# Attention and dense layers with urgent chains, and reciprocals spread to features by DMA

## The chip, the cores and the metric

The kernel runs on one core of one Trainium2 chip. The metric is the device time of one execution in microseconds (us). The kernel before takes 293.84 us, the median of three runs (293.66 to 294.12). TensorE multiplies matrices, VectorE (DVE) and ScalarE (ACT) work on elements, GpSimd (POOL) does small jobs, and SyncE (SP) issues DMAs. Each engine runs its instructions in order and waits on semaphores for the others. Matmuls write to PSUM, which has 8 banks of 128 x 512 f32.

## The reference

x is 2048 tokens by 512 features, bf16. Two blocks alternate, A, B, A, B, with the same weights both times:

```python
x = x + _A_ref(_layernorm(x), wqkv, wo)   # linear attention, 32 heads of 16
x = x + _B_ref(_layernorm(x), w1, w2)     # relu(x @ w1) @ w2, hidden 1376

# _A_ref:
phi = lambda t: jnp.where(t > 0, t + 1, jnp.exp(t)) + 1e-6
pq, pk = phi(q), phi(k)
kv = einsum("bhsd,bhse->bhde", pk, v);  z = einsum("bhsd->bhd", pk)
num = einsum("bhqd,bhde->bhqe", pq, kv)
den = einsum("bhqd,bhd->bhq", pq, z)[..., None] + 1e-6
return (num / den) @ wo
```

The layer norm has no weights and an epsilon of 1e-5.

## The kernel before, in words

Tokens are 16 tiles of 128, in four chunks of four tiles. Everything stays in SBUF: the f32 residual `xres`, the normalized `xn`, its transpose `Tb`, and `big`, which holds phi(k), phi(q) and later the hidden layer.

An attention layer has these parts. `a_k` multiplies `Tb` by wk for a tile and `phi_evac` (L502) evicts it: ScalarE writes x + 1 (L506) and exp (L508), VectorE takes the minimum with 1 (L510) and the maximum of both (L516). `a_q` does the same for q, but transposed: features in partitions, 512 tokens of a chunk in columns. `a_z` sums phi(k) by matmuls with a column of ones. `a_g` accumulates xn^T phi(k) in four banks (`g`), evicted as `GT`; `a_kv` turns this into k^T v with the weights wv, so v itself is never computed. `a_m` masks it to the heads' blocks (`KVT`, L582) and multiplies by wo, which gives the 512 x 512 matrix `Mf`, evicted in four parts (L589). `a_fin` then makes an output tile with four matmuls, phi(q) by `Mf`, and `resid` (L534) adds it to the residual and sums it; L540 on ScalarE sums its squares.

The division is done on phi(q), before `a_fin`. `a_den` (L602) multiplies by `Zc`, so that the denominators of 32 heads lie in 32 rows for each j (of four groups of 128 features), and ScalarE forms the reciprocal as exp(-ln), `rdc` (L608, L610). Only 8 of the 32 rows of a group are heads of it. `a_pqs` (L613) spreads a reciprocal to its head's 16 features with a matmul by a 0/1 matrix, `Esel`, four matmuls of 32 rows for a chunk into four banks, and VectorE multiplies phi(q) by that bank (L619). `Esel` itself is made once at the start by `head_rows` (L427).

A dense layer has `b_h` (10 slices of 128 hidden features for a chunk, relu at L641), `b_hl` for the last 96 features, and `b_group`, in which a group of four tiles begins with matmuls of 32 rows (`w2l`) and goes on with ten for each tile (`w2`).

The norm between layers is `ln_chunk` (L442): four small VectorE operations, a power on GpSimd (L459), one more on VectorE (L461), and `ln_norm` (L464) on ScalarE, VectorE or GpSimd. The transposes of a chunk are one DMA transpose issued by SP (L480), which waits for the four tiles' norms and, the first time, for all loads. Chunk 0 of the dense layers, and chunks 0 and 1 of the first, are transposed on TensorE instead (L485), so that the next layer can begin earlier.

The order is not written out by hand. `layer_steps` lists the steps of each layer and interleaves the end of one layer with the start of the next; every operation goes into a graph with its reads, writes and an assumed duration, and `_list_schedule` (L117) simulates the engines and picks for each, within a window of its next operations, the one that can start first (ties by program order). It also hands out the eight PSUM banks. Operations that may run on several engines (`add_flex`) go where they would end first. The result is a fixed list of instructions for each engine. The assumed durations (L16 to L38) therefore change the order, though not the work.

Of the kernel before, what the change touches and what calls it, by code (L numbers as in the profile page):

```python
# [16 lines left out]
C_MM128 = 58.0  # L17
# [14 lines left out]
C_POOL_POW = 1000.0  # L32
C_POOL_NORM = 900.0
C_SP_ISSUE = 60.0
TAIL = {PE: 70.0, ACT: 230.0, DVE: 80.0, POOL: 300.0, SP: 0.0}
SYNC_LAT = 40.0
LN_EXP_SET = 6
WINDOW = {PE: 64, ACT: 80, DVE: 80, POOL: 12, SP: 6}  # L38


class _Op:
    __slots__ = ("eng", "emit", "reads", "writes", "dur", "lat", "sdeps", "odeps", "idx",
                 "seq", "dma", "name", "t_start", "t_done", "issued", "pos", "nsucc", "alts")
# [19 lines left out]
class _Graph:  # L63

    def __init__(self):
        self.ops = []
        self.last_w = {}
        self.readers = {}
        self.tile_ops = {}
        self.ntiles = 0  # L70

# [5 lines left out]
    def add(self, eng, emit, reads=(), writes=(), dur=100.0, lat=0.0, dma=False, name=""):  # L77
        op = _Op(eng, emit, tuple(reads), tuple(writes), dur, lat, dma, name)
        op.idx = len(self.ops)
        deps = {}  # L80
# [36 lines left out]
def _list_schedule(ops, tile_ops, vbank, nbanks=8):  # L117
# [15 lines left out]
    pend = {e: [o for o in ops if e in engs_of(o)] for e in ENGINES}  # L133
# [4 lines left out]
    remaining = len(ops)  # L138

    def ready_time(o):  # L140
        t = 0.0
        for d in o.sdeps:
            if d.t_done is None:
                return None
            if d.t_done + SYNC_LAT > t:
                t = d.t_done + SYNC_LAT
        for d in o.odeps:
            if not d.issued:
                return None
        need = alloc_of.get(o.idx)  # L150
        if need:
            fr = sorted(x for x in bank_free if x is not None)
            if len(fr) < len(need):
                return None
            tb = fr[len(need) - 1] + SYNC_LAT
            if tb > t:
                t = tb
        return t

    while remaining:  # L160
        best = None
        for e in ENGINES:
# [33 lines left out]
            if cand is not None and (best is None or cand[0] < best[0] - 1e-9  # L196
                                     or (abs(cand[0] - best[0]) <= 1e-9 and cand[1].idx < best[1].idx)):
                best = cand
# [45 lines left out]
def build_kernel(nc, A_x, A_wqkv, A_wo, B_w1, B_w2, out, n_layers_pairs=2, K_STT=0, Q_STT=0, A_PE_CHUNKS=1, windows=None,  # L244
                 WARM=16, SPLIT0=True, TAIL_SPLIT=True, LAST_HALVES=True, FIRST_PE_CHUNKS=2,
# [22 lines left out]
    with es:  # L268
# [15 lines left out]
        NL = 2  # L284
        lnd = sb("lnd", [128, NL, 512], F32)
# [3 lines left out]
        Esel = sb("Esel", [128, 128], BF16)  # L289
# [11 lines left out]
        nm2 = sb("nm2", [128, NT], F32)  # L301
        var = sb("var", [128, NT], F32)
# [6 lines left out]
        veps0 = sb("veps0", [128, 1], F32)  # L309
        rstd0 = sb("rstd0", [128, 1], F32)  # L310
        nbias0 = sb("nbias0", [128, 1], F32)
# [28 lines left out]
        def dma(emit, reads, writes, xfer_ns, name):  # L340
# [5 lines left out]
            op = g.add(SP, _emit, reads, writes, dur=C_SP_ISSUE, lat=xfer_ns, dma=True, name=name)  # L346
# [23 lines left out]
        def h_keys(c):  # L370
            return [("big", il * RU + c) for il in range(4)]
# [3 lines left out]
        def ld_x(t, lo=0):  # L375
            dma(lambda e, t=t: e.dma_start(xin[:, 4 * t + lo:4 * t + 4, :], x_v[:, 4 * t + lo:4 * t + 4, :]),
                [], [("xin", i) for i in range(4 * t + lo, 4 * t + 4)], 1500.0 * (4 - lo) / 4.0, "ld_x%d" % t)
        dma(lambda e: e.dma_start(xin[:, 0, :], x_v[:, 0, :]), [], [("xin", 0)], 450.0, "ld_x0a")
        wq_v = A_wqkv.rearrange("(c p) n -> p c n", p=128)
        ld_x(0, 1)  # L380
        dma(lambda e: e.dma_start(wqkv[:, :, D:2 * D], wq_v[:, :, D:2 * D]), [], [("wk",)], 1500.0, "ld_wk")  # L381
        dma(lambda e: e.dma_start(wqkv[:, :, 0:D], wq_v[:, :, 0:D]), [], [("wq",)], 1500.0, "ld_wq")  # L382
        for t in range(1, NCH):
            ld_x(t)
# [36 lines left out]
        ones_v = onesf[:, :].rearrange("p (j r) -> p j r", r=32)  # L421
        g.add(POOL, lambda e: e.affine_select(hm1[:], ones_v, [[0, 4], [-16, 32]], ALU.is_ge, 0.0, base=0, channel_multiplier=1),
              [("onesf",)], [("hm1",)], 350, name="as_h1")
        g.add(POOL, lambda e: e.affine_select(hm128[:], hm1[:], [[0, 4], [16, 32]], ALU.is_ge, 0.0, base=15, channel_multiplier=-1),
              [("hm1",)], [("hm128",)], 350, name="as_h2")

        def head_rows():  # L427
            b = alloc_bank()
            g.add(PE, lambda e: e.transpose(psv[:, b, 0:64].bitcast(BF16), hm128[:].rearrange("p j r -> p (j r)"), ident[:]),
                  [("hm128",), ("ident",)], [("ps", b)], C_MM128, name="trh")  # L430
            g.add(DVE, lambda e: e.tensor_copy(Esel[:], psv[:, b, 0:64].bitcast(BF16)), [("ps", b)], [("Esel",)], 200.0, name="esel")
# [6 lines left out]
        def ln_stats_first(i):  # L438
            g.add(DVE, lambda e: e.bn_stats(bst[:, i, :], xin[:, i, :]), [("xin", i)], [("bst", i)], C_DVE_BNST, name="bnst%d" % i)  # L439
            g.add(DVE, lambda e: e.bn_aggr(mv[:, i, :], bst[:, i, :]), [("bst", i)], [("mean", i), ("var", i)], C_DVE_SMALL, name="bnag%d" % i)  # L440

        def ln_chunk(t, first):  # L442
            sl = slice(4 * t, 4 * t + 4)
            tl = range(4 * t, 4 * t + 4)
            if first:
                mean_ap = mv[:, sl, 0]
                g.add(DVE, lambda e: e.tensor_scalar(veps[:, sl], mv[:, sl, 1], 0.0, EPS, ALU.max, ALU.add),
                      [("var", i) for i in tl], [("veps", t)], C_DVE_SMALL, name="veps%d" % t)
            else:
                mean_ap = mean[:, sl]  # L450
                g.add(DVE, lambda e: e.tensor_scalar(mean[:, sl], s1[:, sl], INV_D, None, ALU.mult),
                      [("s1", i) for i in tl], [("mean", i) for i in tl], C_DVE_SMALL, name="mean%d" % t)
                g.add(DVE, lambda e: e.scalar_tensor_tensor(nm2[:, sl], mean[:, sl], -1.0, mean[:, sl], ALU.mult, ALU.mult),
                      [("mean", i) for i in tl], [("nm2", t)], C_DVE_SMALL, name="nm2_%d" % t)
                g.add(DVE, lambda e: e.scalar_tensor_tensor(var[:, sl], s2[:, sl], INV_D, nm2[:, sl], ALU.mult, ALU.add),
                      [("s2", i) for i in tl] + [("nm2", t)], [("var", i) for i in tl], C_DVE_SMALL, name="var%d" % t)
                g.add(DVE, lambda e: e.tensor_scalar(veps[:, sl], var[:, sl], 0.0, EPS, ALU.max, ALU.add),  # L457
                      [("var", i) for i in tl], [("veps", t)], C_DVE_SMALL, name="veps%d" % t)
            g.add(POOL, lambda e: e.tensor_tensor(rstd[:, sl], veps[:, sl], nhalf[:, 0:4], ALU.pow),  # L459
                  [("veps", t), ("nhalf",)], [("rstd", t)], C_POOL_POW, name="rstd%d" % t)  # L460
            g.add(DVE, lambda e: e.scalar_tensor_tensor(nbias[:, sl], mean_ap, -1.0, rstd[:, sl], ALU.mult, ALU.mult),  # L461
                  [("mean", i) for i in tl] + [("rstd", t)], [("nbias", t)], C_DVE_SMALL, name="nbias%d" % t)

        def ln_norm(i, first):  # L464
            t = i // 4
            k = tile_of(i)
            src = xin[:, k, :] if first else xres[:, k, :]
            skey = ("xin", k) if first else ("xres", k)
            rd = [skey, ("rstd", t), ("nbias", t)]
            alts = [(ACT, lambda e: e.activation(xn[:, i, :], src, ACTF.Identity, scale=rstd[:, i:i + 1], bias=nbias[:, i:i + 1]),  # L470
                     C_ACT_SB_AP),
                    (DVE, lambda e: e.tensor_scalar(xn[:, i, :], src, rstd[:, i:i + 1], nbias[:, i:i + 1], ALU.mult, ALU.add),  # L472
                     C_DVE_NORM_BF if first else 460.0)]
            if not first:
                alts.append((POOL, lambda e: e.tensor_scalar(xn[:, i, :], src, rstd[:, i:i + 1], nbias[:, i:i + 1], ALU.mult, ALU.add),
                             C_POOL_NORM))
            g.add_flex(alts, rd, [("xn", i)], name="norm%d" % i)

# [23 lines left out]
        def phi_evac(b, dst_ap, dst_key, name, stt):  # L502
            s = scr_state["e"]
            scr_state["e"] = (s + 1) % NSCR
            if not stt:
                g.add(ACT, lambda e: e.activation(dst_ap, psv[:, b, :], ACTF.Identity, bias=1.0 + 1e-6, scale=1.0),  # L506
                      [("ps", b)], [dst_key], C_ACT_PSUM, name=name + "_lin")
# [4 lines left out]
            if stt:  # L512
                g.add(DVE, lambda e: e.scalar_tensor_tensor(dst_ap, psv[:, b, :], 1.0 + 1e-6, emscr[:, s, :], ALU.add, ALU.max),
                      [("ps", b), ("emscr", s)], [dst_key], C_DVE_PSUM, name=name + "_phi")
            else:
                g.add(DVE, lambda e: e.tensor_tensor(dst_ap, dst_ap, emscr[:, s, :], ALU.max),  # L516
                      [dst_key, ("emscr", s)], [dst_key], 340.0, name=name + "_phi")
# [25 lines left out]
        def a_k(i):  # L543
# [3 lines left out]
            phi_evac(b, pk_tile(i), ("big", pk_unit(i)), "k%d" % i, stt=(i % 4) < K_STT)  # L547

        def a_z(i, ZB):
# [4 lines left out]
            mm_group(mk, [("big", pk_unit(i)), ("ones1",)], [("ps", ZB)], 4 * C_MMTINY, "z%d" % i)  # L554
# [5 lines left out]
        def a_g(m, i0, GB):  # L560
# [7 lines left out]
            mm_group(mk, [("xn", i) for i in range(i0, i0 + 4)] + [("big", pk_unit(i)) for i in range(i0, i0 + 4)],  # L568
                     [("ps", GB)], 4 * C_MM512, "g%d_%d" % (m, i0 // 4))

        def a_g_evac(m, GB):
            g.add_flex([(ACT, lambda e: e.activation(GT[:, m, :], psv[:, GB, :], ACTF.Identity), C_ACT_PSUM),
                        (DVE, lambda e: e.tensor_copy(GT[:, m, :], psv[:, GB, :]), C_DVE_FLEX)],
                       [("ps", GB)], [("GT", m)], name="gev%d" % m)

# [5 lines left out]
        def a_m(KB):  # L581
# [393 lines left out]
```

## Time and profile before

| | |
|---|---|
| Median of the runs | 293.84 us (293.66 to 294.12) |
| Profiled execution | 294.0 us, of which the span, from first to last instruction, is 292.3 us |
| Granted TensorE clock | 0.999 |
| TensorE busy | 283.3 us, 97% |
| VectorE, ScalarE, GpSimd busy | 153.4, 172.5, 31.8 us |
| Idle time in front of matmuls, by what ended it | VectorE's memset of the warm-up 1.2, ScalarE's Tb 1.1, Mf 0.8, VectorE's big 0.4, its xn 0.3 us; 1.3 us in eight short pieces with no wait shown |
| DMA | 15.97 MB; all loads have landed by 24.87 us |

The profile is of one execution. Busy times are of instructions, so an engine that waits inside a long one looks busy, and TensorE's matmuls overlap: the mean of one is 379 ns, while the next starts 216 ns after it. The starts in the timeline are therefore a better measure than the sums. "Idle before" is what the engine waited for in front of a group; idle time of an engine that does not set the end costs nothing.

### The profile page before, as it was taken

The numbers are of one execution on the slowest core, as the hardware profiler recorded it, in microseconds if no ns is written. First come the engines' busy times: TensorE is split into PE (matmuls) and PEld (weight loads), VectorE is DVE, ScalarE is ACT, GpSimd is POOL, SyncE is SP. The second block draws the span as 40 slices with busy tenths as digits, with TensorE's granted clock in tenths as the row PEclk, the third lists the DMA queues.
The fourth block names the chain that finished last, engine by engine and source line by source line (L and its number), as shares of the span: only waits on it lengthen the run. The fifth ranks groups of instructions, "written<-read, shape, count | busy, mean of one in ns | idle before, by whom it ended". The sixth has DMA issues, their size and how long they took to land.

```text
span 292.3 us, 4292 instructions
## 1 busy us (share of the span) xinstructions
PE 283.3 (97%) x1649; PEld 128.7 (44%) x1670; DVE 153.4 (52%) x438; ACT 172.5 (59%) x354; POOL 31.8 (11%) x42
## 2 busy tenths in 40 slices
PE   7899999999999999999999999999999999999996
PEld 3354444334444444444444443444444444444443
DVE  5899774999940000347464758928994000022223
ACT  2998596687866664335644899258786766300000
POOL 3102100002430000022020300000243000000000
PEclk9999999999999999999999999999999999999999
DMA  7995320000370000030303400000038000001222
GB/s 222 357 374 107 63 27 0 2 0 0 72 147 0 0 2 0 3 72 11 61 2 72 72 3 0 2 0 0 3 64 152 1 2 0 2 9 63 72 74 72
DMA packets 33780, 15.97 MB, mean 55 GB/s; under 512 B 25312, under 2 KB 33248, under 8 KB 33760
## 3 DMA queue, kind: packets, MB, share of 16 engines
q1 hardware_dynamic: 33760, 15.70, 21.8%
q8 instruction: 13, 0.21, 0.3%
q14 instruction: 7, 0.06, 0.1%
HBM read 7.31 MB, written 2.10 MB: 32 GB/s over the span
## 4 chain that ended last, share of the span: by engine, by line
PE 88%; DVE 6%; DMA 2%; ACT 2%; issue 1%; SPq 1%
PE ps L523 87%; DMA xin<-in_A_x_dram 2%; DVE big L619 2%; DVE xn L472 1%; DVE xres L534 1%; ACT Mf L589 1%; ACT big L506 1%; PE ps L494 0%; DVE bst L439 0%; DVE big L516 0%; DVE emscr L510 0%; ACT sqscr L540 0%; SPq L382 0%; ACT escr L508 0%; SPq L381 0%
## 5 line engine op out<-in xcount | busy, mean ns | idle before, releaser
L523 PE MATMUL ps<-Tb,w 128*128 128x512 bf16 (+1 forms) x416 | 75.0, 379 | 0.0
L523 PE MATMUL ps<-w,big 128*128 128x512 bf16 (+1 forms) x321 | 69.2, 372 | 1.3 <-issue 1.3
L641 ACT ACTIVATE big<-ps 128x512 bf16<-128x512 f32 x78 | 46.5, 596 | 19.6 <-PE ps L523 19.6
L523 PEld LDWEIGHTS ps<-Tb,w 128*128 128x128 bf16 (+1 forms) x416 | 33.5, 97 | 41.2 <-ACT big L641 1.7
L523 PEld LDWEIGHTS ps<-w,big 128*128 128x128 bf16 x330 | 31.4, 98 | 37.6 <-issue 2.3
L534 DVE SCALAR_TENSOR_TENSOR xres<-ps,xres 128x512 f32<-128x512 f32 x32 | 21.8, 687 | 47.2 <-PE ps L523 46.9
L540 ACT ACTIVATE sqscr<-xres 128x512 bf16<-128x512 f32 x48 | 29.9, 629 | 27.5 <-DVE xres L534 27.3
L506 ACT ACTIVATE big<-ps 128x512 bf16<-128x512 f32 x64 | 40.9, 643 | 7.6 <-PE ps L523 7.3
L508 ACT ACTIVATE escr<-ps 128x512 bf16<-128x512 f32 x64 | 41.3, 661 | 0.4 <-DVE emscr L510 0.4
L531 DVE TENSOR_TENSOR xin<-ps,xres 128x512 bf16<-128x512 f32 x15 | 10.4, 692 | 54.5 <-PE ps L523 54.5
L459 POOL TENSOR_TENSOR rstd<-veps,nhalf 128x4 f32<-128x4 f32 x15 | 16.1, 1072 | 175.9 <-DVE veps L457 155.8
L523 PE MATMUL ps<-Tb,wqkv 128*128 128x512 bf16 x128 | 30.6, 379 | 0.0
L523 PE MATMUL ps<-wqkv,Tb 128*128 128x512 bf16 x124 | 28.8, 379 | 1.5 <-ACT Tb L498 1.1
L523 PE MATMUL ps<-Mf,big 128*128 128x512 bf16 x126 | 28.9, 380 | 1.1 <-ACT Mf L589 0.8
L523 PE MATMUL ps<-big,xn 128*128 128x512 bf16 x124 | 29.7, 379 | 0.3
L516 DVE TENSOR_TENSOR big<-big,emscr 128x512 bf16<-128x512 bf16 x64 | 26.5, 422 | 1.2
L510 DVE TENSOR_SCALAR emscr<-escr 128x512 bf16<-128x512 bf16 x64 | 18.5, 296 | 12.3 <-ACT escr L508 12.1
L619 DVE TENSOR_TENSOR big<-big,ps 128x512 bf16<-128x512 bf16 x32 | 19.9, 680 | 1.3 <-PE ps L523 1.3
L523 PEld LDWEIGHTS ps<-wqkv,Tb 128*128 128x128 bf16 x128 | 12.1, 98 | 16.0 <-ACT Tb L498 1.5
L523 PEld LDWEIGHTS ps<-Mf,big 128*128 128x128 bf16 x128 | 11.9, 98 | 16.2 <-ACT Mf L589 1.3
L523 PEld LDWEIGHTS ps<-big,xn 128*128 128x128 bf16 x128 | 11.5, 97 | 13.1 <-issue 1.5
L523 PEld LDWEIGHTS ps<-Tb,wqkv 128*128 128x128 bf16 x128 | 11.5, 97 | 12.3 <-DVE big L619 0.4
(71 smaller groups left out, 184.6 us busy)
## 6 DMA issues: line engine op xcount, KB each, us to landing
wqkv<-in_A_wqkv_dram SPq DMA_DIRECT2D x3, 512.0 KB, 6.1
xin<-in_A_x_dram SPq DMA_DIRECT2D x3, 512.0 KB, 8.0
out_dram<-xin SPq DMA_DIRECT2D x3, 512.0 KB, 2.9
w<-in_B_w_dram SPq DMA_DIRECT2D x1, 1376.0 KB, 11.0
w<-in_B_w_dram SPq DMA_DIRECT2D x1, 1280.0 KB, 13.7
wo<-in_A_wo_dram SPq DMA_DIRECT2D x1, 512.0 KB, 8.8
xin<-in_A_x_dram SPq DMA_DIRECT2D x1, 384.0 KB, 3.3
w2l<-in_B_w_dram SPq DMA_DIRECT2D x4, 96.0 KB, 7.6
```

The source lines that it names most:

```text
L459: g.add(POOL, lambda e: e.tensor_tensor(rstd[:, sl], veps[:, sl], nhalf[:, 0:4], ALU.pow), [("veps", t), ("nhalf",)], [("rstd", t)], C_POO ...
L472: (DVE, lambda e: e.tensor_scalar(xn[:, i, :], src, rstd[:, i:i + 1], nbias[:, i:i + 1], ALU.mult, ALU.add), C_DVE_NORM_BF if first else 4 ...
L506: g.add(ACT, lambda e: e.activation(dst_ap, psv[:, b, :], ACTF.Identity, bias=1.0 + 1e-6, scale=1.0), [("ps", b)], [dst_key], C_ACT_PSUM, ...
L508: g.add(ACT, lambda e: e.activation(escr[:, s, :], psv[:, b, :], ACTF.Exp), [("ps", b)], [("escr", s)], C_ACT_EXP, name=name + "_exp")
L510: g.add(DVE, lambda e: e.tensor_scalar(emscr[:, s, :], escr[:, s, :], 1.0, 1e-6, ALU.min, ALU.add), [("escr", s)], [("emscr", s)], C_DVE_B ...
L516: g.add(DVE, lambda e: e.tensor_tensor(dst_ap, dst_ap, emscr[:, s, :], ALU.max), [dst_key, ("emscr", s)], [dst_key], 340.0, name=name + "_ ...
L523: last = e.matmul(o, l, r, start=st, stop=sp, skip_group_check=skip)
L531: g.add(DVE, lambda e: e.tensor_tensor(xin[:, i, :], psv[:, b, :], src, ALU.add), [("ps", b), skey], [("xin", i)], C_DVE_PSUM, name="resid ...
L534: g.add(DVE, lambda e: e.scalar_tensor_tensor(xres[:, i, :], psv[:, b, :], 0.0, src, ALU.add, ALU.add, accum_out=s1[:, si:si + 1]), [("ps" ...
L540: g.add(ACT, lambda e: e.activation(sqscr[:, q, :], xres[:, i, :], ACTF.Square, accum_out=s2[:, si:si + 1]), [("xres", i)], [("sqscr", q), ...
L619: g.add(DVE, lambda e, j=j, u=u: e.tensor_tensor(unit_ap(u), unit_ap(u), psv[:, bs[j], :], ALU.mult), [("ps", bs[j]), ("big", u)], [("big" ...
L641: g.add_flex([(ACT, lambda e: e.activation(h_evac_ap(c, t), pin(), ACTF.Relu), C_ACT_PSUM), (DVE, lambda e: e.tensor_scalar(h_evac_ap(c, t ...
```

## The change

Seven things change together.

- The reciprocals are spread by DMA. The rows that `a_den` makes now hold each of a group's 8 heads four times (`hm128` repeats a head in 4 columns), so 32 rows hold 8 heads. `a_spread` copies each row to four partitions, four DMAs for a chunk into `rdx`, which has room for two chunks. `a_pqs` multiplies SBUF by SBUF. `head_rows`, `Esel` and the spreading matmuls go.
- The steps around the attention's middle (`bar`) are written in another order, with `a_den`, `a_spread` and `a_pqs` apart from each other and the q chunks between them.
- The output tiles of chunk 0 are made together by `a_fin4`, j outermost.
- Operations can be urgent: `g.urg` moves an operation ahead in the ranking of its engine (not on TensorE). The evictions of `GT`, the mask and `Mf`, the chain of chunk 0's norm and the last chunk's chain have it. One PSUM bank is held in reserve for the next operation in program order that needs one.
- `b_group` is split, and the `w2l` matmuls of the next group are put ahead of the last tile of the one before. Keys of `big` are now for quarters of a unit, so an output tile waits only for its own chunk's relu.
- The small operations of `ln_chunk` are all on GpSimd; the norms are on VectorE, with ScalarE as the alternative for the last two of a chunk. In the first chunk each tile has its own deviation, from Ln and Exp on ScalarE; in the others of the first layer the fourth norm is on ScalarE.
- The loads: x in pieces of 1, 1, 2 and 4 tiles, then wq, with wk issued by ScalarE; 12 warm-up matmuls instead of 16.

```diff
-C_POOL_POW = 1000.0
-C_POOL_NORM = 900.0
+C_POOL_POW0 = 420.0
+C_POOL_POW1 = 145.0
+C_POOL_SMALL = 150.0
...
+        op.urg = self.urg if eng != PE else 0
...
+    def rank(o):
+        return o.idx - o.urg
+    ranked = sorted(ops, key=rank)
...
+            if o is not hd and len(fr) < len(need) + min(RESERVE, len(alloc_of[hd.idx])):
                 return None
...
+        ld_x(0, 1)
+        ld_qk(D, "wk", ACT)
+        ld_x(1, 2)
+        ld_x(2, 4)
+        ld_x(4, 8)
+        ld_qk(0, "wq")
...
+        def ln_rstd_act(i):
+            g.add(ACT, lambda e: e.activation(veps[:, i:i + 1], mv[:, i, 1:2], ACTF.Ln, bias=EPS, scale=1.0),
...
+            g.add(ACT, lambda e: e.activation(rstd[:, i:i + 1], veps[:, i:i + 1], ACTF.Exp, scale=-0.5),
...
+        def ln_chunk(t):
...
+            g.add(POOL, lambda e: e.tensor_scalar(mean[:, sl], s1[:, sl], -INV_D, None, ALU.mult),
+            g.add(POOL, lambda e: e.tensor_tensor(nm2[:, sl], mean[:, sl], mean[:, sl], ALU.mult),
+            g.add(POOL, lambda e: e.tensor_scalar(ex2[:, sl], s2[:, sl], INV_D, None, ALU.mult),
+            g.add(POOL, lambda e: e.tensor_tensor(var[:, sl], ex2[:, sl], nm2[:, sl], ALU.subtract),
+            g.add(POOL, lambda e: e.tensor_scalar(veps[:, sl], var[:, sl], 0.0, EPS, ALU.max, ALU.add),
+            g.add(POOL, lambda e: e.tensor_tensor(rstd[:, sl], veps[:, sl], nhalf[:, 0:4], ALU.pow),
+            g.add(POOL, lambda e: e.tensor_tensor(nbias[:, sl], mean[:, sl], rstd[:, sl], ALU.mult),
...
+        def a_spread(t):
+            for j in range(4):
+                dma(lambda e, j=j: e.dma_start(rdx[:, t % NRD, j, :], rdc[32 * j:32 * j + 32, t, :].unsqueeze(1).broadcast_to([32, 4, 512])),
+                    [("rdc", t)], [("rdx", t % NRD, j)], 500.0, "rdx%d_%d" % (t, j), issue=600.0)
...
-            bs = [alloc_bank() for _ in range(4)]
-            mm_group(lambda: [(psv[:, bs[j], :], Esel[32 * j:32 * j + 32, :], rdc[32 * j:32 * j + 32, t, :], True, True, False) for j in range(4)],
...
-                g.add(DVE, lambda e, j=j, u=u: e.tensor_tensor(unit_ap(u), unit_ap(u), psv[:, bs[j], :], ALU.mult),
+                g.add(DVE, lambda e, j=j, u=u: e.tensor_tensor(unit_ap(u), unit_ap(u), rdx[:, t % NRD, j, :], ALU.mult),
...
+        def a_fin4(t, first_layer):
+            bs = [alloc_bank() for _ in range(4)]
+            for j in range(4):
+                u = pq_unit(j, t)
+                for il in range(4):
...
                 def o_step(il):
-                    b_group(il, last_layer)
+                    b_main(il, last_layer, 0, 3)
+                    if il < 3:
+                        b_small(il + 1, last_layer)
+                    b_main(il, last_layer, 3, 4)
```

## Prediction

> **What bounds the kernel now.** I read the page's busy shares first, then the chain that ended last, then TensorE's groups by shape, then the timeline around each stretch in which the chain leaves TensorE.
>
> ```profile
> PE 283.3 (97%) x1649; PEld 128.7 (44%) x1670; DVE 153.4 (52%) x438; ACT 172.5 (59%) x354; POOL 31.8 (11%) x42
> ...
> PE 88%; DVE 6%; DMA 2%; ACT 2%; issue 1%; SPq 1%
> ```
>
> TensorE is the bound for the whole span, at a granted clock of 0.999. Full 128x512 matmuls start every 0.216 us (the 16 K matmuls at 134.38 are followed at 137.83: 3.45 / 16). So only two things can shorten this kernel: fewer TensorE instructions, and less waiting in front of them. The waits are few. What follows sums them and the removed matmuls.
>
> **1. The reciprocal's spreading leaves TensorE.** Eight groups of four 32-row matmuls (`rdx` in `a_pqs`) go.
>
> ```profile
> 49.20 1.03 PE L523 MATMUL ps<-big,xn 128*128 128x512 bf16 x4
> ...
> 50.16 0.39 PE L523 MATMUL ps<-rdc,Esel 32*128 32x512 bf16 x4
> ...
> 50.49 0.40 PE L523 MATMUL ps<-GT,wqkv 128*128 128x128 bf16 x4
> ```
>
> The first column is the start. Four matmuls from 49.20 would end their turn at 49.20 + 4 x 0.216 = 50.06; the group starts at 50.16 and its successor at 50.49. One group costs 50.49 - 50.06 = 0.43 us, not four times 0.216: the four run side by side. Another group (Mf x12 at 63.05, group at 65.75, Mf at 66.08) gives 66.08 - (63.05 + 2.59) = 0.44. Eight groups: **-3.4 us**, if TensorE is never waiting there; in 47 to 57 us it is busy 9.95 of 10.00.
>
> Against that, the denominators (`den`) are split finer. One alone costs 0.33 + 0.09 = 0.42 us (62.72 to 63.05), two together 0.55 + 0.09 = 0.64 (178.64 to 179.19), three 0.77 + 0.09 = 0.86 (47.34 to 48.11). The built order has 2+1+1 instead of 3+1 in layer one (1.48 against 1.28) and 1+1+1+1 instead of 2+1+1 in layer three (1.68 against 1.48): **+0.4 us**.
>
> On VectorE the multiply that follows reads SBUF (like L516, 0.42 us) instead of PSUM (L619, 0.68): 32 x 0.26 = 8.3 us less work beside TensorE, worth nothing by itself.
>
> **2. The spread's new wait.** Now 32 DMAs of 128 KB do it, four for each chunk, issued by SP. No such copy is in the trace. The nearest rows:
>
> ```profile
> Tb<-xn SPq DMA_TRANSPOSE x12, 4.3
> xin<-in_A_x_dram SPq DMA_DIRECT2D x1, 128.0 KB, 2.2
> out_dram<-xin SPq DMA_DIRECT2D x1, 128.0 KB, 1.7
> ```
>
> The last number is us from issue to landing. The two of equal size bound it at 1.7 and 2.2, and I take 2.0; the transpose (also SBUF to SBUF, four times the bytes) is the far end, 4.3. An issue takes 0.4 to 0.5 us of SP (0.39 and 0.41 for the first two loads), so four land over 1.35 us. The page "DMA: Bandwidth & Descriptors" of the Trainium skill (section "Anatomy of one DMA") gives 2.0 us plus bytes over 436 GB/s for the software-generated path; that would be 2.3 us here, an estimate from that page, and would leave every sum below as it is.
>
> Behind these waits stand VectorE's other instructions, since it runs in order. In layer one the built order has five multiplies (chunk 0, and the first of chunk 1) ahead of the KVT mask. With den at 0: Ln and Exp for two chunks are done at 2.2 and 2.7 (47.34, then 48.90 plus two Exps in 1.16), chunk 0 is issued 2.3 to 3.65 and chunk 1 from 4.1; its first part lands at 6.1, multiplied by 6.5. The mask's input, the last kv group, is ready at 7.1 (54.4 before), and eight Q matmuls (1.73 us) cover the mask (0.69 plus some 0.2 of signals): cover left 0.8. So landings up to 2.0 + 0.6 + 0.8, about 3.4 us, cost nothing. Layer three has the first two of chunk 2 ahead of the mask; den 2 to kv end is 4.8 us there, the second lands at 1.5 + 0.45 + 2.0 = 4.0: the same margin. SP's queue holds no transpose between these DMAs in the built order. Cost at 2.0: **0**.
>
> **3. The Mf stall in layer one.**
>
> ```profile
> 57.05 2.06 ACT L589 ACTIVATE Mf<-ps 128x512 bf16<-128x512 f32 x4
> ...
> 57.33 1.04 PE L523 MATMUL ps<-Tb,wqkv 128*128 128x512 bf16 x4
> ...
> 59.16 3.63 PE L523 MATMUL ps<-Mf,big 128*128 128x512 bf16 x16 [0.79 <-ACT Mf L589]
> ```
>
> ScalarE evicts all four Mf alone, and the first output group needs all four: TensorE, done with Q at 57.33 + 0.86 = 58.19, starts at 59.16. Now two go to VectorE with priority, and `a_fin4` runs chunk 0 by j, so it needs Mf one at a time, 0.86 us apart. The stall goes: **-1.0 us**. Layer three has none there (Q 196.54 x8, Mf 198.27).
>
> **4. The normalization behind that.** Running by j finishes all four tiles at the end T. VectorE's four residual adds (0.69 + 0.08 each) end at T + 2.7, the last square at T + 3.6. The statistics are now on GpSimd. Its elementwise operations on 128x4 are not in the trace: a memset of that size took 0.10; the power took 0.56 at one, 0.86 at three and 1.01 at four elements, so 0.41 plus 0.15 each. Ends 0.10 and 0.41, I take 0.2, nearest the 0.16 of VectorE's same operations. Three of them and the power (1.01) and signals give T + 5.4; norm 0, behind nine residual adds of which the last ends near T + 5.7, ends at T + 6.2; TensorE, with den and 28 matmuls (0.42 + 6.05), wants it at T + 6.5. The fourth norm is on ScalarE (0.81) behind an eviction, about T + 8.4, and the last chunk's multiplies end near T + 9.1 where TensorE is free at T + 8.7. I book 0.6 us of waits for each layer where the trace has 0.26 and 0.28 (70.4 and 209.5): **+0.6 us** for both. At 0.10 for an operation this is 0.3 less, at 0.41 it is 0.6 more, in each layer.
>
> The page "GPSIMD Engine Reference" of the Trainium skill (its introduction) speaks against this move: it calls GpSimd the wrong choice for ordinary elementwise work, with VectorE about twice as fast. Twice 0.16 would be 0.32 an operation, by my estimate 0.4 us more in each layer; the trace shows GpSimd only with powers, memsets, selects and norms.
>
> In the dense layers the same chain feeds DMA transposes that TensorE reaches late: K of layer three starts at 134.4, 142.45, 158.9 and 169.7, the landings are at 131.6, 141.5, 158.2 and 168.7. Slack 0.7 to 3 us hides a chain up to 0.7 longer, and nbias no longer waits behind a residual add (0.69 at 125.08). Cost **0**; uncovered, 0.6 for each of two chunks.
>
> **5. The start.**
>
> ```profile
> 1.23 5.46 PE L407 MATMUL ps<-wrm 128*128 128x512 bf16 x16 [1.23 <-DVE wrm L400]
> ...
> 4.14 0.56 POOL L710 TENSOR_TENSOR rstd<-veps,nhalf 128x1 f32<-128x1 f32 x1 [1.64 <-DVE veps L708]
> ...
> 4.53 1.29 DVE L439 BATCH_NORM_STATS2 bst<-xin 128x6 f32<-128x512 bf16 x2 [0.47 <-DMA xin<-in_A_x_dram]
> ...
> 6.38 0.14 DVE L712 SCALAR_TENSOR_TENSOR nbias<-mv,rstd 128x1 f32<-128x1 f32 x1
> ...
> 6.60 0.38 DVE L714 TENSOR_SCALAR xn<-xin,rstd,nbias 128x512 bf16<-128x512 bf16 x1
> ...
> 7.04 0.40 PE L494 MATMUL ps<-ident,xn 128*128 128x128 bf16 x4 [0.35 <-DVE xn L714]
> ```
>
> The deviation of tile 0 is ready at 4.70, but VectorE is in the statistics of other tiles until 6.38. The new order puts norm 0 ahead of them and takes the deviation from ScalarE (two operations like L399, 0.20): norm 0 near 4.9. Warm-up then binds: 12 instead of 16 matmuls, the last at 5.45, free at 5.7. The transposes start at 5.7 instead of 7.04: -1.3 us, and K needs wk, which landed at 6.05 and still shares the same first 1 MB of loads. ScalarE issues wk itself, ahead of its table load (1.28 us at 1.04); at 0.5 us that is hidden, since it idles until 7.48 here. The gain must survive the transposes of chunks 2 and 3, which wait for all loads (last landing 24.87): chunk 2 can land at 24.9 + 4.3 = 29.2, and TensorE would ask at 31.8 - 1.3 = 30.5. It survives: **-1.3 us** (0 to -2). ScalarE, 9.43 busy of 10.1 us here, gets three norms more.
>
> **6. A wait in layer three** (the `ones` matmuls at 164.32 and 164.99, 0.14 + 0.55 us behind L516) loses its cause, GpSimd and VectorE norms ahead of L516 on VectorE: **-0.6**, with 0 as the other end.
>
> `b_small` and `b_main` move the 32-row groups but keep their number: 0.
>
> **Sum:** -3.4 + 0.4 - 1.0 + 0.6 - 1.3 - 0.6 = **-5.3 us**. The profiled execution took 294.0 (span 292.3, 1.7 around it), so 288.7; it lay 0.16 above the median of 293.84, so **288.5**. Bounds against this sum: -0.7 to +1.3 at the start (2 or 0 gained), -0.1 to +0.6 in term 6, -1.1 (no wait at all) to +1.2 in term 4. All at one end, they give 286.6 and 291.6.
>
> **Rivals.**
> (a) The freed TensorE time comes back as waits for ScalarE and VectorE in the attention layers, since ScalarE is 12.4 of 13.0 busy in 165 to 178. Half of term 1 and the start are lost: +1.7 +1.3, 291.5. Against it: in 178 to 196, where the groups stand, ScalarE is at 8.9 of 18.
> (b) The change does not do what it says: the spread only trades TensorE groups for stalls (landing near 4.3). The mask is then late by 0.9 and the last chunk by 1.0 in each layer, 3.8 together: 292.3.
> (c) **Slower**: the same wait, further. A landing of 7.6 us, as the four 96 KB loads of w2l show in a full queue, delays mask and last chunk by 4.2 and 4.3 in each layer, +17: 305. It beats the gain of 5.3 from a landing of about 4.7 us (1.3 for each of four places). Against it: the queue is empty there (DMA 0 in 57 to 75 us).
>
> **Chances:** forecast 0.66, (a) 0.14, (b) 0.12, (c) 0.08. The range holds the forecast's bounds and (a): 286.6 to 291.8. A measurement of this kernel can tell about 0.2% (0.6 us) from no change. Faster 0.89 (forecast, (a) and most of (b)), same 0.03, slower 0.08.
>
> **What would show it.** No Esel group on TensorE and 1649 - 32 - 1 - 4 = 1612 matmuls; K's first matmul near 6.8; rdx landings under 3.4 us; no idle time of `Mf,big` behind Mf; TensorE's waits for xn or for big near 1 us in all. The prediction is wrong if rdx heads the list of VectorE's waits and TensorE waits behind KVT, or if GpSimd's small operations take 0.4 us.

## The result and the profile after

| | before | after |
|---|---|---|
| Median of the runs | 293.95 us (293.66 to 294.12) | 290.19 us (289.18 to 290.21) |
| Profiled execution, and its span | 294.0 and 292.3 us | 290.21 and 288.5 us |
| Last matmul starts | 289.39 us | 285.56 us |

The ratio is 0.9864 (95% interval 0.9847 to 0.9882): the changed kernel is 3.8 us faster, where 5.3 was forecast. The forecast of 288.5 is 1.7 us too low; its range, 286.6 to 291.8, holds the result. Where an execution was over 1.5% slower than the fastest of its kernel (one of e5 below), medians and ratios leave it out.

From the page of the changed kernel, the busy shares and the row of the new copies (the last number is us from issue to landing):

```profile
PE 281.9 (98%) x1633; PEld 128.2 (44%) x1633; DVE 137.7 (48%) x381; ACT 176.8 (61%) x367; POOL 38.3 (13%) x99
...
rdx<-rdc SPq DMA_DIRECT2D x32, 128.0 KB, 2.6
```

TensorE still bounds everything. The forecast expected 1612 matmuls, from 1649 before; but that page has 1670 weight loads, so 21 matmul records were missing there, and 1670 - 37 = 1633 is the forecast count. The copies land in 2.6 us (2.0 was taken, 3.4 was the limit); issuing one costs SP 0.6.

The list of TensorE's waits in the changed kernel (us in total, times, longest):

```profile
PE ps L429 <- DVE wrm L422: 1.2, 1, 1.2
PE ps L530 <- DVE xn L507: 1.0, 2, 0.7
PE ps L559 <- ACT Tb L534: 0.7, 1, 0.7
PE ps L559 <- ACT escr L544: 0.3, 1, 0.3
PE ps L559 <- DVE big L661: 0.3, 1, 0.3
PE ps L530 <- ACT xn L500: 0.2, 1, 0.2
```

Mf (0.8 before) is gone from it, and the KVT mask is not on it. `escr`, `rdx`'s multiply (L661) and ScalarE's norm (L500) are new, and the wait for the norms at the start (xn) has grown from 0.3 to 1.0. The timeline around the mask and Mf in layer one:

```profile
54.16 0.68 DVE L621 TENSOR_TENSOR KVT<-ps,bmask 128x512 bf16<-128x512 f32 x1
...
55.13 1.03 PE L559 MATMUL ps<-wo,KVT 128*128 128x512 bf16 x4
...
55.91 1.11 ACT L628 ACTIVATE Mf<-ps 128x512 bf16<-128x512 f32 x2
55.97 1.28 DVE L629 CAST Mf<-ps 128x512 bf16<-128x512 f32 x2
55.99 1.03 PE L559 MATMUL ps<-Tb,wqkv 128*128 128x512 bf16 x4
56.85 3.40 PE L559 MATMUL ps<-Mf,big 128*128 128x512 bf16 x15
```

None of TensorE's rows has a wait in brackets: Q, wo, Q and the output follow each other 0.86 us apart. The mask stood behind five multiplies that waited for copies, and was still in time. The start is the other story:

```profile
13.22 2.19 POOL L465 TENSOR_TENSOR rstd<-veps,nhalf 128x4 f32<-128x4 f32 x1 [10.18 <-DVE veps L463]
15.44 0.73 DVE L507 TENSOR_SCALAR xn<-xin,mv,rstd 128x512 bf16<-128x512 bf16 x2 [0.91 <-POOL rstd L465]
...
15.91 0.29 PE L530 MATMUL ps<-ident,xn 128*128 128x128 bf16 x2 [0.67 <-DVE xn L507]
```

In the kernel before, the same stretch had these rows:

```profile
13.25 2.75 PE L523 MATMUL ps<-Tb,wqkv 128*128 128x512 bf16 x12
13.86 1.31 POOL L459 TENSOR_TENSOR rstd<-veps,nhalf 128x4 f32<-128x4 f32 x1 [5.85 <-DVE veps L447]
15.95 1.37 PE L494 MATMUL ps<-ident,xn 128*128 128x128 bf16 x16
```

GpSimd's power for chunk 1 took 2.19 us (1.31 before, 1.04 to 1.23 later in the changed kernel), and the transposes behind it began at 15.91, against 15.95 before. Nearly all that was won until then was gone: the first Q matmuls were 0.76 ahead (12.49 against 13.25), the first matmul for G 0.15 ahead (21.73 against 21.88).

Stage by stage, from the starts of matmuls in the two traces: start -0.15; three groups, the finer den and the Mf stall up to the first output matmul of layer one -2.16; behind it one more group less its new waits +0.17; dense layer one 0 (59.36 us in both from its first h to K of layer three); from there to the end -1.7, with four groups in it.

### The profile page after: what moved, and what is told of

Same layout as the page of the kernel before. It is cut to its first block, busy times and chain, and to the rows that moved or that the text cites. A ratio compares the mean times of both kernels' runs of the same rounds, so it can differ in the third digit from the quotient of the medians.

```text
span 288.5 us, 4271 instructions
## 1 busy us (share of the span) xinstructions
PE 281.9 (98%) x1633; PEld 128.2 (44%) x1633; DVE 137.7 (48%) x381; ACT 176.8 (61%) x367; POOL 38.3 (13%) x99
## 4 chain that ended last, share of the span: by engine, by line
PE 90%; DMA 3%; DVE 2%; ACT 2%; SPq 1%; POOL 1%; issue 0%
PE ps L559 89%; DMA xin<-in_A_x_dram 2%; DVE bst L457 1%; DMA rdx<-rdc 1%; ACT sqscr L576 1%; POOL rstd L465 1%; PE ps L530 1%; SPq L655 1%; DVE xn L507 0%; SPq L393 0%; ACT lnd L648 0%; ACT big L542 0%; ACT rdc L650 0%; DVE mv L459 0%; ACT escr L544 0%
## 5 line engine op out<-in xcount | busy, mean ns | idle before, releaser
L559 PE MATMUL ps<-w,big 128*128 128x512 bf16 (+1 forms) x330 | 71.1, 373 | 0.0
L570 DVE SCALAR_TENSOR_TENSOR xres<-ps,xres 128x512 f32<-128x512 f32 x32 | 21.2, 689 | 49.4 <-PE ps L559 49.4
L544 ACT ACTIVATE escr<-ps 128x512 bf16<-128x512 f32 x64 | 40.6, 650 | 0.0
L559 PE MATMUL ps<-wqkv,Tb 128*128 128x512 bf16 x128 | 30.0, 379 | 1.0 <-ACT Tb L534 0.7
L559 PE MATMUL ps<-big,xn 128*128 128x512 bf16 x128 | 30.3, 379 | 0.0
L479 POOL TENSOR_SCALAR mean<-s 128x4 f32<-128x4 f32 x12 | 3.7, 309 | 148.2 <-DVE xres L570 147.9
L496 DVE TENSOR_SCALAR xn<-xres,mean,rstd 128x512 bf16<-128x512 f32 x36 | 17.9, 543 | 5.4 <-POOL rstd L489 5.1
L661 DVE TENSOR_TENSOR big<-big,rdx 128x512 bf16<-128x512 bf16 x32 | 13.3, 420 | 9.8 <-DMA rdx<-rdc 9.6
```

Of the source, the lines that this page charges most:

```text
L479: g.add(POOL, lambda e: e.tensor_scalar(mean[:, sl], s1[:, sl], -INV_D, None, ALU.mult), [("s1", i) for i in tl], [("mean", i) for i in tl ...
L496: alts = [(DVE, lambda e: e.tensor_scalar(xn[:, i, :], xres[:, k, :], mean[:, i:i + 1], rstd[:, i:i + 1], ALU.add, ALU.mult), 460.0)]
L544: g.add(ACT, lambda e: e.activation(escr[:, s, :], psv[:, b, :], ACTF.Exp), [("ps", b)], [("escr", s)], C_ACT_EXP, name=name + "_exp")
L559: last = e.matmul(o, l, r, start=st, stop=sp, skip_group_check=skip)
L570: g.add(DVE, lambda e: e.scalar_tensor_tensor(xres[:, i, :], psv[:, b, :], 0.0, src, ALU.add, ALU.add, accum_out=s1[:, si:si + 1]), [("ps" ...
L661: g.add(DVE, lambda e, j=j, u=u: e.tensor_tensor(unit_ap(u), unit_ap(u), rdx[:, t % NRD, j, :], ALU.mult), [("rdx", t % NRD, j)] + bk(u), ...
```

## The experiments

The theory after the result: TensorE bounds the kernel, the spread is worth nearly what its groups cost, and the start failed through one power on GpSimd. The rivals: the time won on TensorE comes back as waits (then restoring the groups costs little), or the gain is from the new order and its urgent chains. Each comparison is with interleaved runs of the kernel before (medians 294.28 to 294.46); the changed kernel stands at 0.9864.

| run | median us | ratio to before (95%) |
|---|---|---|
| e1 spreading on TensorE again | 292.61 | 0.9936 (0.9913 to 0.9958) |
| e2 DMA spread alone, copies queued too early | 294.51 | 1.0007 (0.9987 to 1.0027) |
| e2b DMA spread alone | 291.77 | 0.9925 (0.9899 to 0.9950) |
| e3 chunk 1's deviation on ScalarE | 288.57 | 0.9805 (0.9781 to 0.9830) |
| e9 old loads | 290.70 | 0.9878 (0.9855 to 0.9902) |
| e4b 8 warm-up matmuls | 291.71 | 0.9907 (0.9885 to 0.9930) |
| e5 each copy twice | 312.26 | 1.0605 (1.0558 to 1.0652) |
| e6 statistics on VectorE | 292.26 | 0.9934 (0.9922 to 0.9946) |
| e7 output of chunk 0 by tiles | 290.03 | 0.9855 (0.9840 to 0.9869) |
| e8 nothing urgent | 290.49 | 0.9867 (0.9854 to 0.9881) |
| e11 e3, K one in four by VectorE | 289.65 | 0.9837 (0.9823 to 0.9850) |
| e12 e11, Q likewise | 290.34 | 0.9862 (0.9849 to 0.9875) |

**The spread undone, and alone (e1, e2, e2b).** In e1:

```diff
-                dma(lambda e, j=j: e.dma_start(rdx[:, t % NRD, j, :], rdc[32 * j:32 * j + 32, t, :].unsqueeze(1).broadcast_to([32, 4, 512])),
+            mm_group(lambda: [(psv[:, bs[j], :], Esel[32 * j:32 * j + 32, :], rdc[32 * j:32 * j + 32, t, :], True, True, False) for j in range(4)],
```

> The changed kernel with the spreading back on TensorE (four 32-row matmuls for each chunk, the multiply reads PSUM), all else as in the changed kernel. Theory (the spread itself is worth eight groups of 0.43 us, and its DMAs cost only part of a short wait at the last chunk): 293.2 us, +3.0 against 290.2; between +2.6 and +3.4. Rival (TensorE's freed time mostly comes back as waits on ScalarE and VectorE, the gain is from the new order): +0.3 to +1.2.

e1 lost 2.1 us by the ratios, 2.4 by the medians and 2.6 by the profiled executions. That is just under the theory's range and well above the rival's. The multiplies now read PSUM and are longer, but no wait of TensorE's in e1 is put down to them. From the first den to the first h it took 27.72 us in layer one (26.55 in the changed kernel, +1.17 for four groups of 0.43), and from the first den of layer three to the last matmul 111.51 (109.89, +1.62). The 0.55 missing in layer one are, but for 0.03, two waits of the changed kernel that e1 has not, 0.37 for a norm of chunk 0 and 0.47 for the last chunk's multiply, less 0.32 that e1's Q matmuls wait for an eviction of Mf.

e2 and e2b add a_spread after a_den in the kernel before, e2b with chunk 2's copies behind chunk 0's multiplies:

```diff
+                        if t < 2:
+                            a_spread(t)
...
                                 a_pqs((n - 3) // 2)
+                            if n == 3:
+                                a_spread(2)
```

> The kernel before with the DMA spread alone: no new order, no GpSimd statistics, no new start. Theory: -3.4 us for the eight groups, given back in part at the last chunk of each attention layer, where the copies follow the denominators directly and land 2.6 to 4.4 us after their issue (den to last multiply some 7.1 us, covered by 24 matmuls and 16 transposes, 6.1 us): about +1.0 in each layer against 0.27 before. Sum 293.9 - 3.4 + 1.5 = 292.0, between 290.8 and 292.8. Rival (the spread needs the new order to be hidden): 293.5 or more. Rival (the order is worth nothing): 290.4 or less.

In e2 the multiplies of chunk 0 waited for chunk 2's copies and took their reciprocals, so that its output is wrong: 294.51, no faster than before. A spread whose copies come too late gives its whole gain back, here partly through TensorE's clock. A row of e2, and two stretches of 3.41 us (after the busy times and counts of PE, PEld, DVE, ACT and POOL comes the granted clock, then DMA):

```profile
70.49 1.94 PE L491 MATMUL ps<-ident,xn 128*128 128x128 bf16 x16 [2.06 <-DVE xn L469]
...
67.49:70.90 3.41, 1.34 (x9) 0.44 (x7) 3.41 (x14) 3.41 (x12) 2.16 (x2) 1.00 0.54 135
70.90:74.31 3.41, 3.34 (x17) 2.02 (x18) 2.18 (x9) 2.54 (x6) 1.02 (x2) 0.50 0.00 0
```

In layer one TensorE waits 2.06 us for chunk 0's norms, and then has half its clock for 3.41 us, which is some 1.7 us of lost matmul time (an estimate, half of 3.41). Nine of e2's twelve executions show the same granted clock, 0.994.

> The kernel before with the DMA spread alone, once more: in the first such run chunk 2's copies were issued ahead of chunk 0's multiplies, which so waited for them and took their reciprocals; now they follow those multiplies. In layer one three multiplies stand ahead of the KVT mask, in place of eight. Theory: -3.4 us for the eight groups, given back at the last chunk of each layer (+0.7 to +1.0 each against before): 292.3 against 293.9, between 291.0 and 293.0, a ratio of 0.990 to 0.997. Rival (the spread pays only with the new order): within 0.2% of before. Rival (order worth nothing): 290.4 or less.

e2b fits the theory: 2.2 to 2.5 us of the change's 3.8 come from the spread alone (the interval of its ratio is 1.5 to 3.0), without the new order.

**The start (e3, e9, e4b).** In e3, for chunk 1 only:

```diff
+                g.add(ACT, lambda e: e.activation(veps[:, sl], mv[:, sl, 1], ACTF.Ln, bias=EPS, scale=1.0),
+                g.add(ACT, lambda e: e.activation(rstd[:, sl], veps[:, sl], ACTF.Exp, scale=-0.5),
```

> The changed kernel, but chunk 1's deviation in layer one comes from two ScalarE operations on 128x4 instead of GpSimd's power, which took 2.19 us there. Theory (the start lost its gain to this power): the transposes of chunk 1 begin near 15.2 instead of 15.91, the first matmul for G 0.7 us earlier than 21.73, and the whole 0.4 to 0.8 us shorter. Rival (the warm-up's cold clock set the start, and what is won at 15 us is lost again to the next chunk's loads): within 0.2 us.

The fastest version, 5.7 us below before and 1.6 to 1.7 below the changed kernel, twice what was expected. Its timeline at the same place:

```profile
12.61 0.27 ACT L777 ACTIVATE rstd<-veps 128x4 f32<-128x4 f32 x1
13.22 1.05 DVE L507 TENSOR_SCALAR xn<-xin,mv,rstd 128x512 bf16<-128x512 bf16 x3
13.69 0.40 PE L530 MATMUL ps<-ident,xn 128*128 128x128 bf16 x4
```

The deviation is there at 12.9 instead of 15.41, and TensorE's row has no wait. The first z matmul comes at 19.77 (20.47) with four K matmuls more before it: 0.70 + 0.86 = 1.56 earlier. Of that 0.83 is the wait for the power, 0.29 a warm-up that ended earlier and 0.26 a shorter wait at the second tile; the last two cannot be put down to the edit. Another 0.55 came in layer one, where the new order leaves no wait at the norms and the last chunk and has one of 0.33 at the mask instead. So only the 0.83 is the power's own price; the rest came with it.

```diff
-        ld_qk(D, "wk", ACT)
-        ld_x(1, 2)
-        ld_x(2, 4)
-        ld_x(4, 8)
-        ld_qk(0, "wq")
+        ld_x(1, 4)
+        ld_qk(D, "wk")
+        ld_qk(0, "wq")
+        ld_x(4, 8)
```

> The changed kernel with the loads of the start as before: tile 0, tiles 1 to 3 in one, wk, wq, chunk 1, all issued by SP. Theory (the new order of loads delays tile 1 from 4.50 to 5.71 and so the second K group): TensorE's idle 0.55 at 8.2 to 8.75 goes, the 12 K matmuls begin near 9.4, but the power of chunk 1 still holds the transposes at 15.9, so the whole gains 0 to 0.3 us. Rival (the loads set the start): -0.5 or more.

e9 gained nothing (0.9878), though its second K group began at 9.70 (9.89 in the changed kernel): the power took 1.99 us and the transposes of chunk 1 began at 15.82. The order of the loads is not what holds the start.

e4b has `WARM=8` for `WARM=12`.

> The changed kernel with 8 warm-up matmuls instead of 12. Theory (past the first K group the start is set by tile 1's load, landed at 5.7, and by chunk 1's power, not by the warm-up): the first K group begins up to 1.2 us earlier than 7.34, the second no earlier than 9.6, the transposes of chunk 1 near 15.9 as before, the whole within 0.3 us of 290.2. Rival (the warm-up sets the start): -0.6 or less. Rival (the clock needs the 12 matmuls and TensorE runs on at 0.427 for longer): +0.5 or more.

The size, 1.3 to 1.5 us more, is that of the rival with the clock; its mechanism was not seen. The profiled execution (290.20) behaves much as the theory said: K at 6.40, transposes of chunk 1 at 15.37, no gain. Its clock was up before the first K group, whose matmuls start 0.22 us apart. But four of the six executions took 291.6 to 292.5, and no profile shows one of them; three of the four have a granted clock of 0.999 or 1.0 over the whole, one 0.988. What fewer warm-up matmuls cost in these stays open.

**The cover of the copies (e5).** Four copies are issued, and each is issued again when its first has landed:

```diff
+                if j == 0:
+                    for k in range(4):
+                        one(e, k).then_inc(sems[k], 16)
+                e.wait_ge(sems[j], 16)
+                return one(e, j)
```

> The changed kernel with each spreading copy made twice, the second only after the first has landed, with the order on every engine but for a few VectorE steps as in the changed kernel. Landings come 2.7 us later, and for layer one's chunk 1, whose copies queue behind chunk 0's on SP, about 6. Theory (the cover of the KVT mask ends at a landing of 3.4 us, and the last chunk has none): wo of layer one 4.8 later behind the mask, of layer three 2.2 later, the last chunks 2.7 and 2.4 later: +12 us, 302, between 298 and 306. Rival (the copies lie off the path, VectorE has slack): less than +2 us.

Layer one waits where the theory said, and the price is far higher: +22 us by the profiled executions (312.26 against 290.21). The fifth multiply, the mask, wo, and the last chunk's output, from e5's timeline:

```profile
59.10 0.42 DVE L673 TENSOR_TENSOR big<-big,rdx 128x512 bf16<-128x512 bf16 x1 [2.69 <-DMA rdx<-rdc]
59.45 0.68 DVE L621 TENSOR_TENSOR KVT<-ps,bmask 128x512 bf16<-128x512 f32 x1
...
60.19 1.89 PE L559 MATMUL ps<-wo,KVT 128*128 128x512 bf16 x4 [4.98 <-DVE KVT L621]
61.87 1.56 PE L559 MATMUL ps<-Tb,wqkv 128*128 128x512 bf16 x4
...
79.29 5.31 PE L559 MATMUL ps<-Mf,big 128*128 128x512 bf16 x16 [3.04 <-DVE big L673]
```

wo waits 4.98 us for the mask (4.8 expected), the last chunk 3.04 for its multiply. What was not expected is behind the waits: four matmuls take 1.7 instead of 0.86, and sixteen 5.31 instead of 3.62. The table by stretches shows why (the granted clock stands where it stood for e2):

```profile
60.00:64.00 4.00, 3.81 (x12) 1.51 (x13) 3.60 (x11) 2.22 (x5) 0.00 (x0) 0.63 0.85 200
76.00:79.00 3.00, 0.26 (x4) 0.08 (x2) 1.78 (x5) 1.59 (x3) 0.67 (x2) 1.00 0.62 151
79.00:84.00 5.00, 4.71 (x14) 1.81 (x15) 4.88 (x15) 2.75 (x9) 0.97 (x5) 0.66 0.49 92
```

The granted clock falls to 0.5, 0.427 us for a matmul, for 3.41 us at a time: from 59.52, in the first wait, and from 80.00, 0.71 us after the end of the second. Of the 11.65 us that layer one's attention takes longer, the two waits are about 8 and this some 3. In layer three the theory had the wrong place: the mask costs only 0.38, but the third den waits 4.83, for a VectorE operation on its q chunk that stands in the queue behind multiplies whose copies have not landed; half rate follows there too, from 202.88.

**Behind chunk 0's output (e6, e7, e8).** In e6:

```diff
-            g.add(POOL, lambda e: e.tensor_scalar(mean[:, sl], s1[:, sl], -INV_D, None, ALU.mult),
+            g.add(DVE, lambda e: e.tensor_scalar(mean[:, sl], s1[:, sl], -INV_D, None, ALU.mult),
```

and so for the other five; only the power stays.

> The changed kernel with the small operations of the statistics (128x4) back on VectorE; the power stays on GpSimd. Theory (on GpSimd they are stretched to 0.34 to 0.85 us beside VectorE, where VectorE takes 0.16, but on VectorE each waits behind a residual add of 0.69): about even, 290.0, between -0.8 and +0.4. Rival (the move is what keeps the norm chain short in the attention layers and the dense layers): +0.8 or more.

I expected no difference; the rival holds: 2.1 us slower, so that the move is worth about 2. From e6's timeline, the first and the last statistic, the power, the first norm and its transposes:

```profile
63.19 0.16 DVE L479 TENSOR_SCALAR mean<-s 128x4 f32<-128x4 f32 x1
...
65.92 0.16 DVE L487 TENSOR_SCALAR veps<-var 128x4 f32<-128x4 f32 x1
...
66.16 1.01 POOL L489 TENSOR_TENSOR rstd<-veps,nhalf 128x4 f32<-128x4 f32 x1 [36.27 <-DVE mean L479]
...
67.77 0.54 DVE L496 TENSOR_SCALAR xn<-xres,mean,rstd 128x512 bf16<-128x512 f32 x1
...
68.36 0.62 PE L530 MATMUL ps<-ident,xn 128*128 128x128 bf16 x8 [0.92 <-DVE xn L496]
```

and from the changed kernel's:

```profile
64.89 1.04 POOL L489 TENSOR_TENSOR rstd<-veps,nhalf 128x4 f32<-128x4 f32 x1
...
65.96 1.46 DVE L496 TENSOR_SCALAR xn<-xres,mean,rstd 128x512 bf16<-128x512 f32 x3
...
66.79 0.64 PE L530 MATMUL ps<-ident,xn 128*128 128x128 bf16 x8
```

Five operations of 0.16 us need 2.9 us on VectorE, because a residual add of 0.68 stands between each two. On GpSimd the same five ran from 63.07 to 64.81, beside the same residual adds, and the power starts 1.3 us earlier, though its chunk's output ended 0.4 later. In e6 TensorE waits 1.08, 0.37 and 0.28 in layer one and 0.56 and 0.87 in layer three; in the changed kernel 0.37 and 0.47, and 0.12 in all. The difference, 2.2 us, is the whole loss.

In e7 chunk 0 uses `a_fin` as the other chunks do.

> The changed kernel with chunk 0's output groups tile by tile instead of by j. Theory (Mf is now evicted by two engines and all four parts are there at 57.3, so running by j hides the last 0.5 us of it; tile by tile frees the first residual 2.6 us earlier and so shortens the 0.84 us of waits at the first norms and the last chunk of layer one): Mf starts 0.5 us later in each attention layer, the later waits shrink by 0.5 to 0.8: 290.4, between -0.4 and +0.8. Rival (running by j is what took the stall of 1.0 away): +1.0 or more.

No difference, as the theory said: 0.60 and 0.35 us of waiting in front of Mf in the two layers, and none at the norms or the last chunk. Running by j moves a wait from one side of the output to the other.

In e8 `URG`, `URG3`, the two priorities of `g.urg` and `RESERVE` are 0.

> The changed kernel without its urgent chains and without the bank kept in reserve (all priorities 0), the rest the same. The orders differ little: the KVT mask still stands behind five multiplies in layer one, the two VectorE evictions of Mf come behind one multiply more, output matmuls and dense matmuls change places in small groups. Theory (the gain is the spread, the Mf eviction on two engines and the GpSimd statistics, none of which need the priorities): 290.4, between -0.2 and +0.9 against 290.2. Rival (the priorities keep the new waits short): +1.2 or more.

0.9867: the urgent chains and the reserved bank, taken together, do nothing that can be measured. e8 also shows how little the end of the warm-up counts:

```profile
6.46 1.04 PE L559 MATMUL ps<-wqkv,Tb 128*128 128x512 bf16 x4 [0.69 <-ACT Tb L534]
...
13.00 2.19 POOL L465 TENSOR_TENSOR rstd<-veps,nhalf 128x4 f32<-128x4 f32 x1 [9.97 <-DVE veps L463]
...
15.69 1.04 PE L530 MATMUL ps<-ident,xn 128*128 128x128 bf16 x12 [0.67 <-DVE xn L507]
```

Its clock rose earlier and its K began 0.88 ahead of the changed kernel's, yet the transposes of chunk 1, behind the same power of 2.19 us, began only 0.22 ahead.

**What ScalarE still holds up (e11, e12).** On e3, with `K_STT=1`, then also `Q_STT=1`.

> The version with chunk 1's deviation from ScalarE, and besides one in four K tiles evicted by ScalarE's exp and one VectorE operation that reads PSUM, in place of two ScalarE operations and one VectorE operation. It takes 0.6 us from ScalarE and adds 0.27 to VectorE for each of 8 tiles. Theory (what is left of TensorE's waits in layer three's K, 0.48 behind escr and 0.2, is ScalarE's load): -0.5 against 288.6, between -0.8 and 0. Rival (ScalarE is only late once, by order): within 0.2 us of it. It loses if VectorE's extra work delays the residuals before a mask: +0.5.

> As the run before, with one in four Q tiles evicted in the same way too: 0.6 us less on ScalarE, 0.27 more on VectorE for 8 more tiles. Theory: the waits left are few, so it adds nothing: between -0.3 and +0.5 against the run before. Rival (ScalarE holds attention back): -0.5 or more.

Both theories fell: e11 is about 0.9 us slower than e3, e12 about 1.7. The wait of 0.48 in layer three's K is still there in e11, with one of 0.85 just behind it, and TensorE's new waits, that one and 0.56 for Mf, are for VectorE. Relief for ScalarE at VectorE's cost does not help. Whether ScalarE's load alone holds attention these two runs cannot tell, since they load VectorE with it.

## Why the prediction was right, and where it was not

| step | forecast | measured, in the profiled executions |
|---|---|---|
| 1 groups and den | -3.4 + 0.4 | 2.2 to 2.5 won alone (e2b), 2.1 to 2.6 lost when undone (e1), new waits included |
| 2 waits at the mask | 0 | 0, in both layers |
| 3 Mf stall | -1.0 | -1.07 (0.96 at Mf, 0.11 just ahead of it) |
| 4 norms, last chunk | +0.6 | +0.58 in layer one, -0.16 in layer three |
| 5 start | -1.3 | -0.15 |
| 6 wait in layer three | -0.6 | -0.69 |
| not forecast | | +0.48, a K matmul of layer three behind escr; +0.20, a `ones` group there (161.38) |

For step 1 the sum takes -3.0: the changed kernel's trace has no group, and its den cost 1.48 and 1.7 as forecast. With it the measured column adds up to -3.8, and the last matmul came 3.83 earlier. The two waits not forecast stand in e1 too (0.47 and 0.19), so they come with the new order, not with the copies; they give back what step 6 won. Against these rows the forecast's gain is 1.5 too large, and 1.15 of it is step 5.

**Step 5 failed, at the sentence that the gain only had to survive the transposes of chunks 2 and 3.** Its first part was right: norm 0 was ready at 4.94 (4.9 forecast). Then the 12 warm-up matmuls started 0.43 us apart to the last and ended at 6.26, not 5.7, since the clock rose only near the twelfth. K began at 7.34 (6.8 forecast, 8.13 before), so 0.79 was still won there, and e8 shows that an earlier rise does not bring the rest back. What the step never looked at is chunk 1: its deviation still came from GpSimd, in 2.19 us, and ate the rest. What stretched the power was not isolated; VectorE was busy for 60% of it here, and throughout the same power before. e3 takes that one power away and the start's gain appears: the first z matmul, with the same K matmuls ahead of it, at 19.77 against 21.47 before, 1.70 earlier, of which 0.55 are the two pieces that e3's edit need not have made. The row that warned was in the trace of before: the same power took 1.31 and 1.65 us in the start and 1.01 everywhere later.

**Step 4 was near in its sum and wrong in what it thought of the move.** It priced GpSimd's statistics by their duration and never as a gain. The duration was well taken (0.20 to 0.25 for most; up to 0.85 at 67), but e6 shows the move saves 2 us, because what counts is the queue that the operation stands in. The Trainium skill's page "GPSIMD Engine Reference" (introduction) has VectorE about twice as fast for ordinary elementwise work. For these operations of four elements in a partition the traces show 0.15 to 0.16 against 0.20 to 0.25 us, 1.3 to 1.6 times, and the slower engine won. The sum of +0.42 hides two parts that differ: +0.58 in layer one, -0.16 in layer three.

**Step 3's size was right, its cause only half.** e7 shows that eviction by two engines leaves 0.60 of the stall, and that running by j removes these only to give as much back behind the output.

**Step 2 held**, with landings of 2.6 for 2.0. Rival (b), which trades groups for stalls, is what e2 shows when copies are queued wrongly. Rival (c) is what e5 shows in kind. The prices of both left out the half rate after a long wait. Rival (a) is refuted by e1: the groups' time did not come back as waits on ScalarE.

## What to carry to other kernels

When one stage gets faster, follow the chain to the next producer that was hidden behind it before counting the gain; here the first chunk was freed and the second chunk's 2 us power was next. Price a small operation by what stands ahead of it on its engine, not by its duration. When a DMA replaces work on the bounding engine, compare its landing with the cover at each place, since a wait of 2 us or more can also cost the clock.

## What the runs showed of the hardware

- After long waits the granted clock fell to 0.5 for 3.41 us at a time, 0.427 us for a matmul instead of 0.216: after waits of 4.98, 3.04 and 4.83 us in e5 and of 2.06 us in e2. After one of 2.04 us in e5 it did not fall. The falls of e5, at 59.52, 80.00 and 202.88, lie 6 and 36 times 3.41 us apart. An inference from these two traces: the clock is set anew at points 3.41 us apart, by how busy TensorE was since the last one. It was busy 0, 0.71 and 0 us in e5 and 1.34 us in e2 in the 3.41 us ahead of the falls, and 1.44 us in the stretch without one (226.77 to 230.18).
- The clock rises at a varying time after the same start at 1.24 us. Warm-up matmuls start 0.43 us apart at first and 0.22 apart from 4.52 us in e8 (after 8), near 5.0 in before, e5 and e6 (after 9) and from 5.76 in e3 (after 11); in the changed kernel and e1 all 12 start about 0.43 apart.
- GpSimd's small operations stretch in some company and not in other. Beside VectorE's residual adds, which read PSUM, a 128x4 operation took 0.20 to 0.24 us and the power 1.04 (63.07 to 65.93). At the next chunk, beside norms and multiplies between SBUF tiles, such operations took up to 0.85, and at the start, beside phi(k)'s evictions, the power 1.18 to 2.19. Which operation of VectorE does it was not tested.
- A copy of 128 KB from SBUF to SBUF that writes each row to four partitions landed in 2.6 us, and its issue held SP for 0.6.
